# Two linear-attention units per batch feeding an ELU feed-forward layer: block 0's exponentials in place, block 1's in four slots, unit 3's loads ahead of the last quarter of W2, and a new written order up to the fourth block

## The chip, the cores and the metric

The kernel runs on one core of a Trainium2 chip. The figure that counts is the device time of one execution in microseconds: the median of three runs of the kernel before is 292.26 us (292.03 to 292.69). All inputs and the output are float32.

Engine names: PE is the matrix engine, PEld its weight loads, ACT the scalar engine (exponentials, copies, relu), DVE the vector engine, POOL the GpSimd engine, SP the engine that only issues transfers. POOL issues transfers too, between its own computations.

## The reference

```python
q_s = exp(q - max(q, -1));  q_s = q_s / sum(q_s, -1)
k_s = exp(k - max(k, 2));   k_s = k_s / sum(k_s, 2)
kv  = einsum('bhsd,bhse->bhde', k_s, v)
x   = einsum('bhsd,bhde->bhse', q_s, kv)      # 8 batches, 8 heads, 576 rows, 64 wide
x   = x.transpose(0, 2, 1, 3).reshape(4608, 512)
h   = x @ w_in                                # 512 x 2048
g   = where(h > 0, h, exp(min(h, 0)) - 1)
out = g @ w_out                               # 2048 x 512
```

## The kernel before, in words

The work has two halves that run at the same time. The attention half goes in 16 **units** (n = 0 to 15); a unit is half the heads of one batch (`load`). It loads q, k and v (576 KB each), takes exponentials on ACT, row sums and reciprocals of q on DVE, the scaled q (`QS`) on POOL or DVE, turns `QS` on PE (`tp`, line 457) for units 0 to 3 or by a transposing transfer (`turn`, line 470) for later ones, multiplies k and v on PE (`kv_mm`, line 507), scales the result into `MBLK` (lines 516, 520) and multiplies again (`ao_parts`, line 550, for units 0 and 1; `ao_mm`, line 538, later). Two copies (`xt`, line 277) put the product into `XT`, the transposed input of the feed-forward half.

The feed-forward half goes in nine **blocks** of 512 tokens (j = 0 to 8). A block's first product (GEMM1, `hg_mm`, line 620) has eight groups g of eight 128x512 matmuls; each group needs its columns of `W1` and fills a pair of PSUM banks, `PS0` to `PS3`. Then `hg` forms the ELU: one ACT exponential of 1024 columns (line 646), and either an ACT relu (648) and a DVE pass (652), or two DVE passes (657, 659). The second product (`out_mm`, line 673) uses `W2` for blocks 0 and 1; blocks 2 to 8 use a seven-product form of it (lines 757, 733 and 806).

In block 0 only, GEMM1's first three groups go quarter by quarter, kc = 0 to 3: kc 0 and 1 need `XT` of unit 0, kc 2 and 3 that of unit 1. `W1` comes in seven transfers on POOL's queue (`load_w1`, line 377): one for each kc of groups 0 to 2 (384 KB), groups 3, 4 and 5 (512 KB each), groups 6 and 7 (1 MB). `W2` comes in four quarters of 1 MB (`load_w2`, line 385).

What sets the order: the program records every operation once, with what it reads and writes; `ORDER` is a table written out by hand or by a solver, one line of operation numbers for each engine, and every engine does its line strictly in that order. A transfer stands in the line of the engine that issues it. Waits on semaphores are derived from reads and writes, so an operation that waits holds everything behind it in its line. `fill` adds spare matmuls on the identity (`spare`, line 892) into the planned gaps of PE ahead of the first GEMM1; each group of them waits for the identity and for the ACT or DVE operation that by the plan ends last before the gap begins.

In blocks 0 and 1 the exponential of a group goes into one of two slots (`ESB`), taken in turn by a counter (`eslot`); the slot is free again when DVE has made `GR` from it. From block 2 on the exponential is written where the result will stand (`GE` is the same memory as `GR`, with another type). The slots lie in the memory that later holds differences of `W2` (`TB`, made by `combos`).

## Time and profile before

| what | value |
|---|---|
| profiled execution, first to last instruction | 290.4 us |
| median of the three timed runs | 292.26 us |
| PE busy | 280.6 us |
| DVE busy | 225.5 us |
| ACT busy | 209.7 us |
| POOL busy | 167.8 us |
| granted PE clock, mean | 0.999 |
| transfers between 5 and 40 us | 355 to 400 GB/s |

The profile gives no time of its own for the profiled execution beyond its span, 290.4 us; the median of the timed runs is 1.9 us more than that. PE is the busiest engine, and the chain of work that ended last runs through PE from 13.8 us to 287.1 us. Busy time of ACT, DVE and POOL counts only where PE waits for them. PSUM results of a matmul come after the start of the next one, so in a timeline a group of matmuls overlaps with the one behind it; the chain gives times that add up.

### The profile page before, as it was taken

The page shows a single profiled execution, that of the slowest core. Times are in us where ns is not written, and L with a number is a line of the kernel's source. Part 1 is how long each engine was busy: PE and PEld are TensorE (multiplying, and loading weights), DVE is VectorE, ACT ScalarE, POOL GpSimd, SP SyncE. Part 2 cuts the span into 40 slices and gives each one's busy share as a digit, 9 for nine tenths or more (in the row PEclk, how much of TensorE's full clock was granted, in tenths as well). Part 3 has the DMA queues.
Part 4 walks back from the last instruction along what each step waited for, and adds up shares of the span by engine and source line. Part 5 has one row for each costly group of instructions (what it writes and reads, how often), then busy time and mean ns, then how long its engine had stood idle before and what let it go on. Part 6 is the DMA issues. An engine that isn't in the chain of part 4 may idle for free.

```text
span 290.4 us, 5465 instructions
## 1 busy us (share of the span) xinstructions
PE 280.6 (97%) x2176; PEld 243.7 (84%) x2176; DVE 225.5 (78%) x425; ACT 209.7 (72%) x237; POOL 167.8 (58%) x161
## 2 busy tenths in 40 slices
PE   2899999999999999999999999999999999999995
PEld 0488787778888899989999988989999999988995
DVE  3758834777699978989996987688977786794884
ACT  4857839989899899968995598975385656665510
POOL 1991335523869778676574886757314234277741
PEclk9999999999999999999999999999999999999999
DMA  7999999798896838739939295313102002300334
GB/s 259 399 363 390 389 389 339 163 260 323 238 349 163 241 91 228 202 78 305 178 96 222 56 292 129 76 40 71 46 18 56 0 2 67 78 2 1 92 73 128
DMA packets 36474, 50.04 MB, mean 172 GB/s; under 512 B 16352, under 2 KB 18144, under 8 KB 36448
## 3 DMA queue, kind: packets, MB, share of 16 engines
q1 hardware_dynamic: 29680, 33.96, 43.7%
q0 software_dynamic: 6528, 15.47, 17.8%
q8 instruction: 17, 0.28, 0.5%
q10 hardware_dynamic: 240, 0.26, 0.3%
q14 instruction: 9, 0.07, 0.1%
HBM read 36.70 MB, written 9.44 MB: 159 GB/s over the span
## 4 chain that ended last, share of the span: by engine, by line
PE 94%; DMA 2%; POOL 2%; SPq 0%; issue 0%; DVE 0%
PE PS L620 46%; PE PS L806 32%; PE PS L673 10%; PE PS L538 3%; DMA KR<-in_k_dram 2%; PE PS L507 2%; POOL W L377 1%; POOL VB L277 0%; PE PS L457 0%; POOL QS L433 0%; SPq L359 0%; PE PS L550 0%; DVE OSB L815 0%
## 5 line engine op out<-in xcount | busy, mean ns | idle before, releaser
L620 PE MATMUL PS<-XT,W 128*128 128x512 f32 x576 | 142.0, 393 | 0.1
L620 PEld LDWEIGHTS PS<-XT,W 128*128 128x128 f32 x576 | 105.0, 188 | 21.2 <-DVE GR L659 0.5
L652 DVE SCALAR_TENSOR_TENSOR GR<-PS,GE 128x512 fp32r<-128x512 f32 x112 | 76.8, 686 | 18.7 <-ACT GE L648 16.7
L646 ACT ACTIVATE GE<-PS 128x1024 f32<-128x1024 f32 x56 | 57.4, 1025 | 40.0 <-PE PS L620 34.2
L757 POOL TENSOR_TENSOR GR<-GR 128x256 fp32r<-128x256 f32 (+1 forms) x48 | 47.2, 996 | 31.5 <-DVE SB L757 16.6
L648 ACT ACTIVATE GE<-GE 128x1024 f32<-128x1024 f32 x56 | 59.4, 1061 | 1.4
L806 PE MATMUL PS<-W,GR 128*128 128x256 f32 x336 | 53.7, 283 | 0.0
L806 PE MATMUL PS<-TB,GR 128*128 128x256 f32 x336 | 51.3, 283 | 0.0
L806 PEld LDWEIGHTS PS<-W,GR 128*128 128x128 f32 x336 | 47.6, 191 | 1.7
L806 PEld LDWEIGHTS PS<-TB,GR 128*128 128x128 f32 x336 | 45.7, 191 | 0.7
L433 POOL TENSOR_TENSOR QS<-QR,RZQ 128x1152 f16<-128x1152 f32 (+1 forms) x16 | 30.4, 1898 | 21.4 <-DVE RZQ L423 19.7
L815 DVE TENSOR_TENSOR OSB<-OSB,PS 128x256 f32<-128x256 f32 x84 | 34.7, 416 | 10.3 <-PE PS L806 9.2
L673 PE MATMUL PS<-W,GR 128*128 128x512 f32 x128 | 32.7, 396 | 0.0
L757 POOL TENSOR_TENSOR GR<-SB,GR 128x256 fp32r<-128x256 f32 (+1 forms) x18 | 17.3, 971 | 24.6 <-PE PS L806 12.7
L673 PEld LDWEIGHTS PS<-W,GR 128*128 128x128 f32 x128 | 23.3, 188 | 5.0 <-DMA W<-in_moe_w_out_dram 0.5
L757 POOL TENSOR_TENSOR SB<-GR 128x256 fp32r<-128x256 f32 (+1 forms) x20 | 19.2, 965 | 13.7 <-DVE GR L652 6.4
L421 DVE TENSOR_REDUCE ZQ<-QR 128x18 f32<-128x1152 f32 (+2 forms) x18 | 21.7, 1207 | 6.1 <-ACT QR L419 4.8
L757 DVE TENSOR_TENSOR GR<-GR 128x256 fp32r<-128x256 f32 (+1 forms) x36 | 21.3, 603 | 0.6 <-PE PS L806 0.6
L277 POOL CAST VB<-VR 128x1152 bf16<-128x1152 f32 (+1 forms) x11 | 11.9, 1084 | 13.1 <-DMA VR<-in_v_dram 13.1
L646 ACT ACTIVATE ESB<-PS 128x1024 f32<-128x1024 f32 x16 | 16.1, 1024 | 4.5 <-PE PS L620 3.4
L399 ACT ACTIVATE KR<-KR 128x1152 bf16<-128x1152 f32 x16 | 18.4, 1155 | 0.8 <-DMA KR<-in_k_dram 0.8
L277 ACT ACTIVATE XT<-PS 128x512 fp32r<-128x512 f32 (+6 forms) x23 | 13.6, 595 | 6.3 <-PE PS L538 3.2
(58 smaller groups left out, 271.4 us busy)
## 6 DMA issues: line engine op xcount, KB each, us to landing
out_dram<-OSB SPq DMA_DIRECT2D x61, 128.0 KB, 2.4
QR<-in_q_dram SPq DMA_DIRECT2D x12, 576.0 KB, 4.9
KR<-in_k_dram SPq DMA_DIRECT2D x12, 576.0 KB, 6.3
VR<-in_v_dram SPq DMA_DIRECT2D x12, 576.0 KB, 5.1
W<-in_moe_w_out_dram POOLq DMA_DIRECT2D x4, 1024.0 KB, 16.7
QR<-in_q_dram POOLq DMA_DIRECT2D x4, 576.0 KB, 12.1
VR<-in_v_dram POOLq DMA_DIRECT2D x4, 576.0 KB, 13.0
KR<-in_k_dram POOLq DMA_DIRECT2D x4, 576.0 KB, 11.1
```

The source lines that it names most:

```text
L277: return e.activation(dst, src, AF.Copy) if e is self.nc.scalar else e.tensor_copy(dst, src)
L399: S.add("act", t_act(1152, False), lambda e: e.activation(ek[:, :, :, :].rearrange("p h c d -> p (h c d)"), flat(k), AF.Exp), key - 2, X=[ ...
L421: S.add("dve", t_dve(m), lambda e, qp=qp, zp=zp: e.tensor_reduce(zp, qp, AX.X, ALU.add), key - 3, R=[f"qR{i}{x}" for x in xs], W=[f"ZQ{i}{ ...
L433: lambda e, qp=q[:, :, a:b, :], rz=rz, dst=qs[:, :, a:b, :]: e.tensor_tensor(dst, qp, rz, ALU.mult),
L620: last = e.matmul(P[:, t * 512:(t + 1) * 512], self.W1[:, kc, tt * 128:(tt + 1) * 128], self.XT[:, kc, rc:rc + BLK], start=(kc == 0), stop ...
L646: S.add("act", t_act(1024, True), lambda e: e.activation(ge, P, AF.Exp), key, W=own, X=banks)
L648: S.add("act", t_act(1024, False), lambda e: e.activation(ge, ge, AF.Relu, bias=1.0, scale=-1.0), key, X=own)
L652: S.add("dve", t_dve(512 if j else 1024), lambda e, u=u: e.scalar_tensor_tensor(*(x[:, :, u, :] if j else x for x in (gt, P)), 0.0, ge[:, ...
L673: last = e.matmul(dst, self.tile(jb, jj, ts), self.W2[:, jj, c0:c1], start=(jj == 0), stop=(jj == 15))
L757: lambda e: e.tensor_tensor(dst, a, b, op), key, R=R, W=W, X=X, after=after)
L806: last = e.matmul(dst, a[i][:, y_, :], b[i][:, y_, :], start=start and i == 0 and y_ == 0, stop=stop and i == len(grps) - 1 and y_ == z - ...
L815: S.add("dve", t_dve(256), lambda e: e.tensor_tensor(dst, a, b, ALU.add), key, R=R, W=W, X=X, after=after)
```

## The change

Five things change in the program, and the table of orders is new up to about the end of block 1 (behind it the table is the old one with every number raised by 4).

1. `hg`: block 0's exponentials, and those of block 1's groups 4 to 7, are written in place into `GE`; block 1's groups 0 to 3 have a slot of their own each (`ESB` has four slots of 4 KB instead of two). Where a place in `GE` still held parts of units 1 and 3 (`early`), the exponential waits for their last readers (`after=users`). `combos` names the two new slots as written.
2. `load_w2` takes any range of `W2`; the loads of unit 3's k and v are recorded ahead of the last quarter of `W2`, which comes in two transfers of 512 KB. `out_mm` of block 0 does the last quarter in two halves.
3. Groups 4 and 5 of `W1` come in one transfer of 1 MB.
4. Unit 3's turn and first product use the bank pair `AB` (PS3), as the other units do; before they used `C` (PS2).
5. `spare_until` is the second `kv_mm` itself.

```diff
-        if j == 1:
-            gw += sorted(set(sum((self.early(u) for u in us), [])))
+        lent = [n for u in us for n in self.early(u)] if j == 1 else []
+        users = [o for n in sorted(set(lent)) for o in S.w.get(n, []) + S.r.get(n, [])]
...
-        own = gw
-        if j < 2:
-            i = self.eslot % 2
-            self.eslot += 1
-            own = [f"E{i}"]
-            ge = self.ESB[i][:, :].rearrange("p (c u t) -> p c u t", c=2, u=2) if j else self.ESB[i][:, :]
-        S.add("act", t_act(1024, True), lambda e: e.activation(ge, P, AF.Exp), key, W=own, X=banks)
+        own, apart = gw, j == 1 and g < 4
+        if apart:
+            own = [f"E{g}"]
+            ge = self.ESB[g][:, :].rearrange("p (c u t) -> p c u t", c=2, u=2)
+        S.add("act", t_act(1024, True), lambda e: e.activation(ge, P, AF.Exp), key, W=own, X=banks, after=users)
...
-        for g0, g1 in ((3, 4), (4, 5), (5, 6), (6, 8)):
+        for g0, g1 in ((3, 4), (4, 6), (6, 8)):
             self.load_w1(g0, g1, range(4), -30)
...
-        self.load_w2(2, -27)
-        self.load_w2(3, -25)
+        self.load_w2(8, 12, -27)
         for t in "kv":
             self.load(3, t, -26)
+        for jj in (12, 14):
+            self.load_w2(jj, jj + 2, -25)
...
-            ps, eng = (C if x == 0 else AB, "both") if n == 3 else (AB, "act")
+            ps, eng = AB, "both" if n == 3 else "act"
...
-                self.out_mm(0, ts, (ts + 2) % 4, 4 * jq, 4 * jq + 4, key)
+                for jj in range(4 * jq, 4 * jq + 4, 2 if jq == 3 else 4):
+                    self.out_mm(0, ts, (ts + 2) % 4, jj, jj + (2 if jq == 3 else 4), key)
...
     "pe": (
-        "35 52 33 37 56 57 54 60 80 78 79 64 65 82 81 84 87 85 88 83 86 89 99 103 110 133 121 107 "
+        "32 34 36 51 55 53 56 59 78 79 80 82 63 64 81 83 84 87 85 88 86 89 99 103 110 133 121 107 "
```

**The first place is PE from its first instruction to the first GEMM1 matmuls.** `PS0<-ID` are the spare matmuls, `QS0` and `QS1_54` the scaled q of units 0 and 1, `VB0,KR0` the `kv_mm` of unit 0. Before:

```order
L892 MATMUL PS0<-ID 128x512 x5
L457 MATMUL PS3<-ID,QS0 128x128 x4
L892 MATMUL PS0<-ID 128x512 x2
L457 MATMUL PS1<-ID,QS1_54 128x128 x5
L892 MATMUL PS0<-ID 128x512
L457 MATMUL PS3<-ID,QS0 128x128 x5
L507 MATMUL PS2<-VB0,KR0 64x65 x36
L892 MATMUL PS0<-ID 128x512 x4
L550 MATMUL PS2<-qsT0,MBLK0 128x512 x2
L457 MATMUL PS1<-ID,QS1_54 128x128 x4
L507 MATMUL PS0<-VB1,KR1 64x65 x36
L620 MATMUL PS2<-XT,W1 128x512 x2
```

After:

```order
L890 MATMUL PS0<-ID 128x512 x6
L457 MATMUL PS3<-ID,QS0 128x128 x5
L890 MATMUL PS0<-ID 128x512 x4
L457 MATMUL PS3<-ID,QS0 128x128 x4
L507 MATMUL PS2<-VB0,KR0 64x65 x36
L457 MATMUL PS1<-ID,QS1_54 128x128 x5
L890 MATMUL PS0<-ID 128x512 x5
L550 MATMUL PS2<-qsT0,MBLK0 128x512
L457 MATMUL PS1<-ID,QS1_54 128x128 x4
L550 MATMUL PS2<-qsT0,MBLK0 128x512
L507 MATMUL PS0<-VB1,KR1 64x65 x36
L620 MATMUL PS3<-XT,W1 128x512 x2
```

Unit 0 is turned as a whole ahead of unit 1, the larger half first; there are 15 spare matmuls instead of 12, and the first group of them waits for the small exponential on ACT that loads the table (line 343) where before it waited for an exponential of unit 0's q. On ACT, the copy of unit 0's second half of `qsT` stands behind the exponential of unit 1's k and the cast of unit 1's v; before, the copies of `qsT` stood ahead of both.

**The second place is POOL's line from the third transfer of W1 on.** Before:

```order
L377 DMA W1<-in_moe_w_in_dram 128x1x768 x2
L377 DMA W1<-in_moe_w_in_dram 128x4x256
L433 TENSOR_TENSOR QS1_54<-QR1,RZQ1 128x2x4x64
L277 CAST VB1<-VR1_56 128x2x4x64
L377 DMA W1<-in_moe_w_in_dram 128x4x256 x2
L377 DMA W1<-in_moe_w_in_dram 128x4x512
L385 DMA W2<-in_moe_w_out_dram 128x4x512
L359 DMA QR0<-in_q_dram 128x2x576
L385 DMA W2<-in_moe_w_out_dram 128x4x512
L359 DMA QR1<-in_q_dram 128x2x576
L359 DMA VR0<-in_v_dram 128x2x576
L359 DMA KR0<-in_k_dram 128x2x576
```

After:

```order
L377 DMA W1<-in_moe_w_in_dram 128x1x768
L433 TENSOR_TENSOR QS1_54<-QR1,RZQ1 128x2x4x64
L359 DMA QR0<-in_q_dram 128x2x576
L377 DMA W1<-in_moe_w_in_dram 128x1x768
L277 CAST VB1<-VR1_56 128x2x5x64
L377 DMA W1<-in_moe_w_in_dram 128x4x256
L377 DMA W1<-in_moe_w_in_dram 128x4x512 x2
L359 DMA VR0<-in_v_dram 128x2x576
L385 DMA W2<-in_moe_w_out_dram 128x4x512
L433 TENSOR_TENSOR QS0<-QR0,RZQ0 128x2x5x64
L385 DMA W2<-in_moe_w_out_dram 128x4x512
L359 DMA KR0<-in_k_dram 128x2x576
```

Unit 2's q is now loaded ahead of the last quarter of `W1`'s first groups (kc 2 comes last), and its v ahead of `W2`; the second quarter of `W2` stands behind a product on POOL that waits for unit 2's reciprocals.

**The third place is ACT in block 0**, from the last copy of `XT` of unit 1 on. `ESB0` and `ESB1` are the two slots, `GE` the memory of the results. Before:

```order
L277 ACTIVATE XT<-PS0 128x512
L646 ACTIVATE ESB0_57<-PS3 128x1024
L646 ACTIVATE ESB1_58<-PS1 128x1024
L648 ACTIVATE ESB1_58<-ESB1_58 128x1024
L646 ACTIVATE ESB0_57<-PS2 128x1024
L646 ACTIVATE ESB1_58<-PS0 128x1024
L648 ACTIVATE ESB1_58<-ESB1_58 128x1024
L646 ACTIVATE ESB0_57<-PS3 128x1024
```

After:

```order
L277 ACTIVATE XT<-PS0 128x512
L395 ACTIVATE QR0<-QR0 128x1152
L644 ACTIVATE GE_50<-PS3 128x1024
L644 ACTIVATE GE_50<-PS1 128x1024
L646 ACTIVATE GE_50<-GE_50 128x1024
L644 ACTIVATE GE_50<-PS2 128x1024
L644 ACTIVATE GE_50<-PS0 128x1024
L644 ACTIVATE GE_50<-PS3 128x1024
L646 ACTIVATE GE_50<-GE_50 128x1024
```

No exponential waits for a slot any more, the relu of group 3 comes behind the exponential of group 4, and the exponential of unit 2's q stands at the front. SP's line is the same in both kernels.

More of the change, by code (lines that the diff above doesn't have):

```diff
@@ L318, in alloc @@
         self.ESB = [at(f"ESB{i}", [128, 1024], F32, offset=tbase + NSP * 1024 + 4096 * i)
-                    for i in range(2)]
+                    for i in range(4)]
         self.OSB0 = [at(f"OSBX{i}", [128, 512], F32, offset=tbase + 2048 * i)
@@ L718, in w2 @@
         z0, z1 = GROUPS[grp]
-        return [f"W2_{s}" for s in range(z0 // 2, (z1 + 1) // 2)]
+        return [f"W2_{s}" for s in range(z0, z1)]
     def combos(self, key, grp):
```

32 lines of the change are left out of this document (16 added, 16 removed), and 136 rows, old and new, of the table ORDER.

## The prediction

> **What bounds the kernel now.** I read the page's busy line and its chain by engine first, then the chain piece by piece, then the first 20 us as a timeline, and last the times from issue to landing of single transfers.
>
> ```profile
> PE 280.6 (97%) x2176; PEld 243.7 (84%) x2176; DVE 225.5 (78%) x425; ACT 209.7 (72%) x237; POOL 167.8 (58%) x161
> PE 94%; DMA 2%; POOL 2%; SPq 0%; issue 0%; DVE 0%
> ```
>
> PE is busy for all but 10 us of the span, and 94% of the chain that ended last is PE. So the end moves by three things only: when PE begins the real work, what it waits for afterwards, and the tail. The pieces of the chain that tell this (start, length, line, number of matmuls):
>
> ```profile
> 13.79 0.49 PE PS L507 x35
> 14.27 1.59 PE PS L620 x6
> 15.86 0.46 PE PS L550 x2
> 16.32 13.16 PE PS L620 x58
> 29.48 0.37 PE PS L538 x4
> 29.85 1.93 PE PS L673 x8
> ...
> 31.80 3.06 PE PS L673 x12
> 34.86 0.52 PE PS L457 x9
> ...
> 39.19 1.05 PE PS L673 x4
> ...
> 42.63 3.67 PE PS L673 x16
> ...
> 48.44 5.57 PE PS L620 x24
> ...
> 54.05 2.11 PE PS L620 x8
> ...
> 58.95 3.91 PE PS L620 x16
> ...
> 74.73 1.81 PE PS L620 x8
> ...
> 271.45 15.60 PE PS L806 x130
> ```
>
> The long pieces give the price of work without waits: 13.16/58 = 0.227 us for a GEMM1 matmul, 3.67/16 = 0.229 us for one of the second product. Against these prices some pieces are too long: the first 20 of line 673 took 1.93 + 3.06 = 4.99 instead of 4.58 (0.41 lost), the four at 39.19 1.05 instead of 0.92 (0.13), the 32 from 48.44 5.57 + 2.11 = 7.68 instead of 7.26 (0.42), the 16 at 58.95 3.91 instead of 3.63 (0.28). Together 1.24 us. From 74.73 on a group of eight takes 1.81 = 8 x 0.227; I find no more waits of PE up to the last piece. The order there is the old one, so a shift of PE at 73 us is carried to the end. What can be won is therefore 1.24 us of waits plus what the beginning gives. The beginning:
>
> ```profile
> 2.03 0.20 ACT L343 ACTIVATE RZK<-RZK 128x2 f32<-128x2 f32 x1
> 4.82 1.26 ACT L419 ACTIVATE QR<-QR 128x512 f32<-128x512 f32 x2 [2.59 <-DMA QR<-in_q_dram]
> 5.49 0.69 DVE L421 TENSOR_REDUCE ZQ<-QR 128x8 f32<-128x512 f32 x1 [3.88 <-ACT QR L419]
> 5.51 2.32 PE L892 MATMUL PS<-ID 128*128 128x512 f16 x5 [5.51 <-ACT QR L419]
> 6.49 1.05 POOL L433 TENSOR_TENSOR QS<-QR,RZQ 128x512 f16<-128x512 f32 x1 [4.62 <-DVE RZQ L423]
> 8.04 1.06 PE L892 MATMUL PS<-ID 128*128 128x512 f16 x2
> 8.93 0.58 ACT L277 ACTIVATE qsT<-PS 128x512 fp32r<-128x512 f16 x1
> 9.39 0.87 POOL L277 CAST VB<-VR 128x512 bf16<-128x512 f32 x1
> 10.19 1.91 POOL L377 DMA_DIRECT2D W<-in_moe_w_in_dram  x3
> 10.82 1.04 PE L892 MATMUL PS<-ID 128*128 128x512 f16 x4
> 12.01 1.17 POOL L433 TENSOR_TENSOR QS<-QR,RZQ 128x512 f16<-128x512 f32 x1
> 12.35 0.73 PE L550 MATMUL PS<-qsT,MBLK 128*128 128x512 f32 x2 [0.49 <-DVE MBLK L520]
> 13.40 0.60 ACT L277 ACTIVATE XT<-PS 128x512 fp32r<-128x512 f32 x1
> ```
>
> And the transfers: two rows in the timeline that issue (start, length), and the answers that give the time from issue to landing of the one transfer in that stretch, in the same order.
>
> ```profile
> 3.58 0.52 SPq L359 DMA_DIRECT2D VR<-in_v_dram  x1
> 17.26 0.80 POOL L385 DMA_DIRECT2D W<-in_moe_w_out_dram  x1
> ```
> ```profile
> VR<-in_v_dram SPq DMA_DIRECT2D x1, 576.0 KB, 8.8
> W<-in_moe_w_out_dram POOLq DMA_DIRECT2D x1, 1024.0 KB, 14.5
> W<-in_moe_w_in_dram POOLq DMA_DIRECT2D x1, 512.0 KB, 6.4
> KR<-in_k_dram POOLq DMA_DIRECT2D x1, 576.0 KB, 4.8
> ```
>
> So unit 1's v lands at 3.58 + 8.8 = 12.4, and the second quarter of W2 at 17.26 + 14.5 = 31.8, just where the chain's piece of twelve begins at 31.80: that is the wait at W2. The third answer is group 5 of W1, the middle one of three issues from
>
> ```profile
> 13.56 2.28 POOL L377 DMA_DIRECT2D W<-in_moe_w_in_dram  x3
> 15.00:20.00 5.00, 5.00 (x23) 4.13 (x22) 1.60 (x3) 2.42 (x3) 5.00 (x8) 1.00 1.75 355
> 20.00:25.00 5.00, 5.00 (x23) 4.13 (x22) 4.60 (x6) 4.68 (x6) 3.23 (x5) 1.00 1.40 388
> ```
>
> issued at 13.56 + 0.76 = 14.3 and landed at 20.7. The two other rows are windows; their last figure is GB/s. The queue is never empty here, so a transfer lands when the bytes ahead of it have passed, at 355 to 388 GB/s: 576 KB cost 1.5 us, 1 MB 2.7. The fourth answer is a load of k at 46 us, when the queue had run low: 4.8 us for bytes worth 1.5, so up to 3.3 us go from issue to first bytes.
>
> **Term 1, the beginning.** GEMM1 starts when both unit 0's XT and unit 1's kv_mm are done. ACT now stands so: unit 1's k, unit 1's v (half of it, 512 columns), then unit 0's second qsT, then XT. The v lands at 12.4 and nothing of that chain can be earlier: cast 0.62 (the mean of the two at 4.82), 13.05; qsT 0.58 (row at 8.93), 13.6; line 550's first matmul needs 0.1 to start and its result is there after 0.73 - 0.23 = 0.5, 14.25; XT 0.60, 14.85; 0.1 to PE: 14.95. Before, the qsT copies lay ahead of the v and XT was ready at 14.0. On POOL: reduce, reciprocal and scaling of the larger half of unit 0 (640 columns, 1.05 x 640/512 = 1.3) end at 8.0; two issues of W1 and the first cast end at 10.25 as before (the cast waits for v, not for them); one issue 0.64 (1.91/3), unit 1's QS 1.05, two issues 1.35 end at 13.3; the cast of 640 columns costs between 0.87 (the row of 512) and 1.09 (that times 640/512), so 14.2 to 14.4, and kv_mm 0.49 behind it ends at 14.7 to 14.9. Both chains meet at 14.95 against 14.27: **0.7 later**, between 0.3 (POOL's cast at its lowest and half of ACT's handovers gone) and 1.7 (the clock, below). Some of the 0.23 that the first six matmuls lost behind kv_mm (1.59 instead of 1.36) should now lie in the wait for XT: 0.1 off.
>
> **Term 2, waits that go.** In block 0 the exponentials and in block 1 the slots no longer wait for DVE; unit 3's k and v come early enough that nothing in 38 to 48 us waits for them; the last quarter of W2 comes in halves. With this the 0.13, 0.42 and 0.28 go: 0.83 us. They were lost in the copies and slots ahead of block 1's first groups, and I follow the new order by hand to 73 us without a wait above 0.1 (the copies of XT behind unit 3's reduce, the turn of unit 3 behind a copy of PS3: 0.1 together). Bounds: nothing to all of it.
>
> **Term 3, transfers that now come later.** Ahead of W2's second quarter now pass unit 2's q (as before) and its v (new): 31.8 + 1.5, less 0.25 for 1 MB of W1 in longer rows (1 MB at 388 instead of 355), makes 33.0. PE wants it at 14.95 + 64 x 0.227 + 0.46 + 0.37 + 8 x 0.229 + 0.52 = 32.65 (blocks 0's GEMM1, two small products, eight matmuls, a turn). So of the 0.41 lost there before, 0.35 stay. Its issue on POOL stands behind the scaling of unit 2's q, which needs a reciprocal that DVE does behind group 1: 25.1 by the same prices, and the bytes ahead of it last until 28.5, and its own come by 25.1 + 3.3 = 28.4, so the queue just doesn't run dry. Groups 4 and 5 of W1 in one transfer, with unit 2's q ahead: 20.7 + 1.5 - 0.25 = 21.95; PE wants group 4 at 14.95 + 32 x 0.227 + 0.46 = 22.65. Before, group 4 had its own transfer and some 3 us in hand; now it has 0.7. A transfer can land later than its bytes say, so this costs nothing to 0.7; I take nothing. The relu of group 3 behind the exponential of group 4 lets PS0 go at 27.9, wanted at 28.15: nothing.
>
> **Term 4.** The cast and copies that move from ACT to DVE cost PE nothing, since DVE has idle time up to 80 us; two more bank uses by unit 3 are in term 2.
>
> **The sum.** +0.7 - 0.1 - 0.83 + 0.1 - (0.41 - 0.35) = -0.2 us: a span of 290.2 against the profiled 290.4, and as the median is 1.9 us above the span, 292.1 against 292.26. A measurement of this kernel can tell about 0.2%, 0.58 us, from no change; this is less.
>
> [...] The spare matmuls before took 0.46 us each at 5.51 and 0.53 at 8.04, and 0.26 at 10.82: PE reaches its full rate between 2.5 and 5.3 us after it begins. After the change the first six wait only for the ACT row that ends at 2.23, run to 5.0, and then PE has nothing until QS at 8.0. Counted from there, full rate comes between 10.6 and 13.4. At the slow rate the five spare matmuls ahead of line 550 run from 12.3; with full rate at 13.4 they end at 13.9 instead of 13.6, and 0.25 is lost, most of which W2's second quarter hides. If it doesn't come before line 550 at all, the five end at 12.3 + 5 x 0.46 = 14.6, line 550 and kv_mm run slow as well (some 0.2), and GEMM1 starts at 16.1; that is rival c. [...]
>
> **The rivals.** (a) *The beginning isn't later.* If the handovers on ACT are shorter and the cast on POOL is at its low price, GEMM1 starts at 14.6, and the transfers are early enough: -0.7, 291.5. For it: every wait in term 1 is 0.05 to 0.1 that I put in. Against: v at 12.4 is fixed. (b) *W1 and W2 late; slower.* Group 4 waits for the joined transfer, or POOL's line holds W2's second quarter behind QS; it decides when the joined transfer lands after 22.65. With 23.5 and a queue that runs dry for 0.5: +0.8, 293.1. For it: group 5 landed 6.4 us after issue, and the transfers wait in one queue; against: the later ones have their bytes in hand. (c) *PE still at half rate when line 550 comes*: GEMM1 at 16.1 instead of 14.95, of which 0.35 is hidden by W2: -0.2 + 0.8 = +0.6, 292.9. Against: the four spare matmuls and the turns behind 8.0 leave PE hardly idle, and 5.3 us sufficed before. (d) *The waits don't go*: what was lost in block 1 wasn't the slots, and 0.7 comes back: 292.8.
>
> **How the numbers follow.** Forecast 0.45 (its own range 291.7 to 292.6), a 0.25, b 0.13, c 0.09, d 0.08. Faster than 291.68 is a and a little of the forecast, 0.28; slower than 292.84 is b, half of c and d, and what I didn't see in an order that is new on all engines: 0.27; the rest, 0.45, is the same. The range takes a at its best (start at 14.6, all 1.24 gone: 291.1) and b at 293.2.
>
> **What would show it.** In the profile of the changed kernel: the first spare matmul at about 2.3 us; the first L620 at 14.9 to 15.2; the first piece of second products beginning at 30.4 and a wait of 0.3 to 0.4 behind the turn of unit 2 at about 33; the first GEMM1 of block 1 at about 48.4; 24 of it without a wait; the same last piece of 130 and the same tail. A first L620 beyond 15.5, a wait ahead of group 4, or pieces in 50 to 62 us that are too long would prove me wrong.

## The result: 293.28 us, slower by 0.31%

| | kernel before | changed kernel |
|---|---|---|
| median, us | 292.15 (291.82 to 292.69, 8 runs) | 293.28 (292.56 to 293.59, 8 runs) |
| ratio | | 1.0031, 95% interval 1.0020 to 1.0042 |
| span of the profiled execution, us | 290.4 | 290.8 |

Predicted were 292.1 us, with a range of 291.1 to 293.2; the time lies just above the range. The execution of the changed kernel that was profiled is the shortest of its eight: the others have spans of 290.9 to 291.8. So its profile shows 0.4 us of the loss of 1.1, and the rest has to be found in what differs from one execution to the next.

The busy line of the page of the changed kernel; PE and DVE are busier than before by 1.1 and 4.5 us, ACT less by 3.5:

```profile
PE 281.7 (97%) x2179; PEld 244.6 (84%) x2179; DVE 230.0 (79%) x430; ACT 206.2 (71%) x231; POOL 171.1 (59%) x162
```

The pieces of its chain (start, length, line, matmuls) that answer to those shown of before. Line 672 is the second product, line 805 the later form of it:

```profile
14.80 8.31 DMA W<-in_moe_w_in_dram
...
23.25 7.55 PE PS L620 x32
...
31.17 1.93 PE PS L672 x8
...
33.61 2.82 PE PS L672 x12
...
49.03 1.86 PE PS L620 x8
50.89 0.47 PE PS L672 x2
51.36 5.44 PE PS L620 x24
...
58.86 2.07 PE PS L620 x8
...
271.79 15.60 PE PS L805 x130
```

Before, 58 matmuls of GEMM1 ran from 16.32 to 29.48 without a break. Now the chain doesn't reach back through PE at 23.25 but into a transfer: the joined one of W1's groups 4 and 5, issued at 14.8 and landed at 23.11. Behind it everything is tight: the second products without a lost 0.4 us (2.82 for twelve), 24 matmuls of block 1 in 5.44 = 24 x 0.227. The last piece begins 0.34 us later than before (271.45), and so it ends.

The first 24 us as a timeline (start, length, engine, line; in brackets the idle time and what ended it):

```profile
2.29 2.74 PE L890 MATMUL PS<-ID 128*128 128x512 f16 x6 [2.29 <-ACT RZK L343]
8.08 0.71 PE L457 MATMUL PS<-ID,QS 128*128 128x128 f16 x5 [3.05 <-POOL QS L433]
12.01 1.54 PE L890 MATMUL PS<-ID 128*128 128x512 f16 x5
14.91 2.12 PE L620 MATMUL PS<-XT,W 128*128 128x512 f32 x8
23.25 7.55 PE L620 MATMUL PS<-XT,W 128*128 128x512 f32 x32 [0.30 <-DMA W<-in_moe_w_in_dram]
```

GEMM1 begins at 14.91, 0.64 later than before. Its first 32 matmuls and line 550 end PE's work at 14.91 + 32 x 0.227 + 0.46 = 22.65 or so; group 4 begins at 23.25, 0.6 later. By the starts of the single matmuls PE was ready at 22.78, so the wait and the slower matmul behind it cost 0.5 to 0.6 us.

### The profile page after: what moved, and what is told of

It is laid out like the page before. It is cut to its first block, busy times and chain, and to the rows that moved or that the text cites. A ratio compares the mean times of both kernels' runs of the same rounds, so it can differ in the third digit from the quotient of the medians.

```text
span 290.8 us, 5462 instructions
## 1 busy us (share of the span) xinstructions
PE 281.7 (97%) x2179; PEld 244.6 (84%) x2179; DVE 230.0 (79%) x430; ACT 206.2 (71%) x231; POOL 171.1 (59%) x162
## 4 chain that ended last, share of the span: by engine, by line
PE 91%; DMA 4%; POOL 3%; DVE 1%; issue 0%; ACT 0%; POOLq 0%
PE PS L620 43%; PE PS L805 32%; PE PS L672 10%; DMA W<-in_moe_w_in_dram 3%; PE PS L538 3%; PE PS L507 2%; DMA QR<-in_q_dram 1%; POOL W L377 1%; POOL QS L433 1%; POOL VB L277 1%; PE PS L457 0%; DVE ZQ L421 0%; ACT QR L419 0%; DVE OSB L814 0%; POOL QR L359 0%
## 5 line engine op out<-in xcount | busy, mean ns | idle before, releaser
L620 PE MATMUL PS<-XT,W 128*128 128x512 f32 x576 | 142.2, 393 | 0.3 <-DMA W<-in_moe_w_in_dram 0.3
L620 PEld LDWEIGHTS PS<-XT,W 128*128 128x128 f32 x576 | 105.0, 188 | 21.2 <-issue 0.7
L650 DVE SCALAR_TENSOR_TENSOR GR<-PS,GE 128x512 fp32r<-128x512 f32 (+1 forms) x120 | 84.4, 704 | 22.6 <-ACT GE L646 20.6
L644 ACT ACTIVATE GE<-PS 128x1024 f32<-128x1024 f32 x68 | 69.5, 1025 | 46.1 <-PE PS L620 40.3
L646 ACT ACTIVATE GE<-GE 128x1024 f32<-128x1024 f32 x62 | 65.8, 1061 | 1.6
L433 POOL TENSOR_TENSOR QS<-QR,RZQ 128x1152 f16<-128x1152 f32 (+2 forms) x17 | 32.7, 1926 | 19.5 <-DVE RZQ L423 17.7
L756 POOL TENSOR_TENSOR GR<-SB,GR 128x256 fp32r<-128x256 f32 (+1 forms) x18 | 17.4, 974 | 24.4 <-PE PS L805 12.7
L277 POOL CAST VB<-VR 128x1152 bf16<-128x1152 f32 (+2 forms) x11 | 12.7, 1157 | 12.1 <-DMA VR<-in_v_dram 9.2
L395 ACT ACTIVATE QR<-QR 128x1152 f32<-128x1152 f32 x14 | 16.2, 1159 | 3.0 <-DMA QR<-in_q_dram 3.0
L277 ACT ACTIVATE OSB<-PS 128x256 f32<-128x256 f32 (+1 forms) x21 | 7.9, 387 | 13.6 <-PE PS L805 13.6
```

The costliest lines, as they stand in the source:

```text
L277: return e.activation(dst, src, AF.Copy) if e is self.nc.scalar else e.tensor_copy(dst, src)
L433: lambda e, qp=q[:, :, a:b, :], rz=rz, dst=qs[:, :, a:b, :]: e.tensor_tensor(dst, qp, rz, ALU.mult),
L620: last = e.matmul(P[:, t * 512:(t + 1) * 512], self.W1[:, kc, tt * 128:(tt + 1) * 128], self.XT[:, kc, rc:rc + BLK], start=(kc == 0), stop ...
L644: S.add("act", t_act(1024, True), lambda e: e.activation(ge, P, AF.Exp), key, W=own, X=banks, after=users)
L646: S.add("act", t_act(1024, False), lambda e: e.activation(ge, ge, AF.Relu, bias=1.0, scale=-1.0), key, X=own)
L650: S.add("dve", t_dve(512 if j else 1024), lambda e, u=u: e.scalar_tensor_tensor(*(x[:, :, u, :] if j else x for x in (gt, P)), 0.0, ge[:, ...
```

## The experiments

All times are medians, each compared with runs of the kernel before on the same chip (medians of 292.01 to 292.12). "Before" and "changed" stand for the two kernels.

### Again, and the spare matmuls

The changed kernel once more, without an edit.

> The changed kernel once more, for a second profile beside the first, whose span of 290.8 us is the shortest of its eight runs (median about 291.5). Theory W (the joined transfer of W1's groups 4 and 5 lands after PE wants it, and by how much differs from run to run): a profile with a longer span shows it landing after 23.1, the wait ahead of line 620's 33rd matmul beyond 0.6 us, and the same first L620 at 14.9. Theory C (the early spare matmuls leave PE idle from 5 to 8 us, and the full rate comes at another moment from run to run): the longer span goes with a lower granted clock, slow 128x512 matmuls (over 0.4 us) later than 13 us and a first L620 at 15.3 to 16. Median time by both 293.0 to 293.5.

Measured: 293.31 us (292.62 to 294.24), ratio 1.0041 [1.0026, 1.0057]; the profiled span is 291.1. The two rows of its chain:

```profile
14.82 8.60 DMA W<-in_moe_w_in_dram
...
23.55 7.58 PE PS L620 x32
```

The first L620 came at 14.93, as in the first profile; the joined transfer landed 0.3 us later, and the span is 0.3 longer. That is what theory W expected.

Next, the spare matmuls of the changed kernel late, as before had them, and those of before early, as the changed kernel has them. In both the edit is the planner's start of the spares:

```diff
-    SPIN_FROM, WARM = 5400.0, 11300.0
+    SPIN_FROM, WARM = 5600.0, 11300.0      # changed kernel, spares late
...
-    SPIN_FROM, WARM = 5400.0, 11300.0
+    SPIN_FROM, WARM = 5200.0, 11300.0      # kernel before, spares early
```

> The changed kernel with its first spare matmuls (five instead of six) behind the first exponential of unit 0's q, as in the kernel before, so that they run from 5.6 to 7.9 us and PE is hardly idle ahead of the first turn at 8.1. Theory C: full rate from about 10.2 us in every run, the spare matmuls at 8.6 take 0.26 us and not 0.46, the spans agree within 0.3 us and the median falls by 0.5 to 0.8 us to 292.5 to 292.8. Theory W: the time stays at 293.1 to 293.4, since GEMM1 begins at 14.9 because of unit 1's v either way and its group 4 still waits.

> The kernel before with its first five spare matmuls behind the small table-loading exponential that ends at 2.2 us, as in the changed kernel: they run from 2.3 to 4.6, then PE is idle to 7.6. Theory C: full rate comes at 12 to 14 us in place of 10.2, later in some runs, GEMM1 begins 0.2 to 1.0 us later and the median rises by 0.3 to 0.9 us to 292.5 to 293.1 with a wider spread. Theory W: no change, 292.0 to 292.3.

Measured: 293.11 us (292.61 to 293.43), ratio 1.0030 [1.0020, 1.0040], for the late spares in the changed kernel; 292.00 us (291.86 to 292.25), ratio 0.9997 [0.9988, 1.0006], for the early ones in before. The timelines of the two, in this order:

```profile
5.84 2.31 PE L890 MATMUL PS<-ID 128*128 128x512 f16 x5 [5.84 <-ACT QR L419]
24.18 7.55 PE L620 MATMUL PS<-XT,W 128*128 128x512 f32 x32 [0.72 <-DVE GR L650]
```
```profile
2.29 2.31 PE L892 MATMUL PS<-ID 128*128 128x512 f16 x5 [2.29 <-ACT RZK L343]
14.14 1.66 PE L620 MATMUL PS<-XT,W 128*128 128x512 f32 x6
```

In before the early spares leave PE idle from 4.6 to 7.55 and GEMM1 begins at 14.14 all the same. So early spares alone cost nothing. In the changed kernel the late spares don't help: the seven runs have granted clocks of 0.998 or more, and the time is 293.11 us. In the 14 executions of the changed kernel the span doesn't follow the granted clock closely either: 290.8 to 292.4 us at 0.998 and more, 290.9 to 292.0 at 0.994, 291.8 and 291.9 in the two at 0.988, where the clock may have a part. As the cause of the loss theory C falls. With the late spares group 4 began as late as 24.18. The row names a DVE pass that ended at 24.10, but that pass freed the bank of group 1, which group 4 doesn't use; the joined transfer, issued at 15.0, landed 9.0 us later, at the same moment.

### The transfers in the changed kernel

W1's groups 4 and 5 apart again:

```diff
-        for g0, g1 in ((3, 4), (4, 6), (6, 8)):
+        for g0, g1 in ((3, 4), (4, 5), (5, 6), (6, 8)):
```

> The changed kernel with W1's groups 4 and 5 in two transfers of 512 KB again. Theory W: group 4 lands by 22.2 us, the wait ahead of it (0.58 us in the profile: 23.25 instead of 22.67) goes; W2's second quarter, landed at 32.7, is then wanted at 33.0, so the gain stays: 292.3 to 292.8 and the time stands 0.5 to 1.0 us below the changed kernel. Theory C: the time doesn't move by more than 0.2 us where the clock came late, and by 0.5 only where it didn't; median 293.0 to 293.3.

Measured: 293.05 us (292.35 to 294.74), ratio 1.0035 [1.0020, 1.0050]. The wait ahead of group 4 is gone, and the time hardly moved. The chain shows why (line numbers are lower by 2 here), and below it stand POOL's rows of the same time:

```profile
17.55 7.46 PE PS L618 x32
...
25.03 1.04 ACT GE L642
...
26.09 1.60 DVE GE L653
27.69 1.14 DVE GR L648
...
28.87 2.12 PE PS L618 x8
```
```profile
25.65 0.81 POOL L383 DMA_DIRECT2D W<-in_moe_w_out_dram  x1
26.45 0.72 POOL L357 DMA_DIRECT2D KR<-in_k_dram  x1
27.16 0.74 POOL L357 DMA_DIRECT2D QR<-in_q_dram  x1
```

The last group of GEMM1 wants the bank of group 3. That is free only when DVE has made group 3's result, and DVE does it behind its pass of group 4 (line 653), which waits for group 4's exponential. That pass took 1.60 us here, against 0.68 in before, while POOL issued three transfers one behind the other. From 17.55 to the end of the last group, 28.87 + 2.12 = 30.99, the 56 matmuls took 13.4 us instead of 56 x 0.227 = 12.7. By the starts of the single matmuls 0.36 us of that are lost ahead of the last group, and 0.15 each ahead of the matmuls at 18.33 and 26.70, which begin right behind landings of W1 (18.29 and 26.57). So a wait of 0.6 us stood in front of others of 0.7, half of it at the bank. The next two kernels put group 3's relu and pass back ahead of group 4's, alone and with the split:

```diff
-    act: ... 96 100 104 101 111 112 ...      dve: ... 98 105 102 106 113 ...
+    act: ... 96 100 101 104 111 112 ...      dve: ... 98 102 105 106 113 ...
```

> The changed kernel with block 0's relu of group 3 on ACT ahead of the exponential of group 4 again, and DVE's pass of group 3 ahead of that of group 4, as in the kernel before. Theory B (two waits lie behind each other in block 0: the joined W1 transfer ahead of group 4, and behind it the bank of group 3, which group 6 wants 24 matmuls later and which is free only 5.3 us after group 4 begins, since the relu of group 3 stands behind group 4's exponential): alone this changes little, since in the changed kernel's profile the bank is free at 28.6 and wanted at 28.7; 0 to 0.3 us less, 293.0 to 293.3. Theory H (the head alone: GEMM1 begins 0.64 us later, and this is carried to the end): no change, 293.2 to 293.4.

> Both at once: W1's groups 4 and 5 in two transfers, and group 3's relu and pass in their old places. Theory B: with the transfers split alone 0.7 us were lost at the bank (58 matmuls' stretch of 12.9 us took 13.6), with both edits no wait is left in block 0's GEMM1, the second products begin at about 30.5 instead of 31.17, and the time falls by 0.5 to 0.9 us to 292.3 to 292.7. Theory H: 293.0 to 293.2, as with the transfers split alone.

Measured: alone 293.32 us (292.87 to 294.40), ratio 1.0045 [1.0027, 1.0062]; both edits 292.69 us (292.36 to 293.29), ratio 1.0018 [1.0008, 1.0028]. This is what theory B expected of the times: each edit alone gives 0 to 0.25, both together 0.6. The interval of both still overlaps those of the changed kernel (1.0020 to 1.0042, and 1.0026 to 1.0057), so the size of the gain is uncertain. The chains of the two:

```profile
14.79 8.86 DMA W<-in_moe_w_in_dram
...
23.78 7.51 PE PS L620 x32
```
```profile
17.70 0.91 PE PS L618 x4
...
18.65 8.46 PE PS L618 x36
...
27.13 3.90 PE PS L618 x16
```

Theory B expected no wait in GEMM1 with both edits, and that isn't so in the execution that was profiled (span 291.2, above the usual 290.9 of this kernel): the pieces at 18.65 and 27.13 begin behind landings of W1, at 18.61 and 26.99, and cost 0.3 us each. The bank isn't waited for any more.

Four profiles so far have group 4 waiting for the joined transfer in the changed kernel's order of transfers. From one to the other the span follows the start of group 4:

| kernel | group 4 begins | span |
|---|---|---|
| changed, first profile | 23.25 | 290.8 |
| changed, again | 23.55 | 291.1 |
| group 3's relu first | 23.78 | 291.3 |
| spares late | 24.18 | 291.6 |

From 22.65, where PE would have been ready in the first profile, this is 0.6 to 1.5 us (in the last two, GEMM1 itself began 0.2 later). The changed kernel's usual span is 291.5. That group 4 begins near 24 us in such a run is read off this table, since none of them was profiled.

### The head pulled forward

Could the 0.64 us of the later beginning be won back? On ACT the copy of unit 0's second qsT ahead of unit 1's k, on POOL the cast of unit 1's v ahead of two issues; once in the changed kernel, once with the two edits above:

```diff
-    act: ... 21 33 22 37 39 35 57 ...      gp: ... 17 47 67 16 38 18 ...
+    act: ... 21 33 22 35 37 39 57 ...      gp: ... 17 47 38 67 16 18 ...
```

> The changed kernel with its head alone pulled forward: on ACT the copy of the second half of unit 0's qsT ahead of the exponential of unit 1's k (it can run at 10.95 instead of 12.9), on POOL the cast of unit 1's v ahead of the issues of unit 2's q and of W1's third quarter (12.45 instead of 13.4). By both theories the first L620 comes at 13.9 to 14.3 instead of 14.91. Theory H: the time falls by 0.5 to 0.8 us to 292.4 to 292.8. Theory B: group 4 then waits the longer for the joined transfer, which isn't earlier (23.1 to 24.0 us, later by up to 0.6 by the later issue), and the time stays at 293.0 to 293.5.

> All three edits: the head pulled forward, W1's groups 4 and 5 in two transfers, group 3's relu and pass in their old places. Theory B: group 4's own transfer (landed at about 22.1 with the transfers split) is now wanted at 21.9 and holds PE up to 0.4 us, and W2's second quarter (32.7 to 33.0) is wanted at 32.3; so the gain over the two edits without the head is 0.1 to 0.4 us: 292.0 to 292.5. Theory H: the head gives its whole 0.6 to 0.9 us: 292.2 to 292.5 from the head alone, whatever the others do.

Measured: 294.08 us (293.47 to 295.63), ratio 1.0078 [1.0053, 1.0103], and 294.32 us (293.01 to 296.64), ratio 1.0086 [1.0058, 1.0115]: both slower, by more than either theory said. The first one's timeline:

```profile
14.55 2.12 PE L620 MATMUL PS<-XT,W 128*128 128x512 f32 x8 [0.60 <-DMA W<-in_moe_w_in_dram]
...
19.96 10.27 PE L620 MATMUL PS<-XT,W 128*128 128x512 f32 x44 [1.91 <-DMA W<-in_moe_w_in_dram]
```

The edit delayed the issue of the last quarter of W1's groups 0 to 2 by 1.2 us (12.85 to 14.03), and it landed 2.0 us later (17.90 to 19.92); PE now waited 1.91 for it. The transfers ran short meanwhile: 147 GB/s between 15 and 16 us, against 349 in the changed kernel. So PE's pace through GEMM1 hangs on when W1 is issued. Theory H is not tested by this, since the edit that pulled the head forward pushed W1 back.

### The moved transfers in the kernel before

The direct test: the two moves of transfers done in the kernel before, and nothing else. Numbers of operations are those of before.

```diff
-    gp: ... 48 40 19 20 21 69 68 70 ...      ((3, 4), (4, 5), (5, 6), (6, 8))
+    gp: ... 48 40 68 19 20 21 69 70 ...      unit 2's q (68) ahead of W1's groups 4 to 7: q alone
+    ((3, 4), (4, 6), (6, 8))                 groups 4 and 5 in one transfer: joined alone
```

> The kernel before with two of the change's moves of transfers alone: unit 2's q is issued ahead of W1's groups 4 to 7, and groups 4 and 5 come in one transfer. Theory Q (the queue: bytes put ahead of W1 and the joined transfer make group 4 late, by how much differs from run to run): group 4 is wanted at 22.0 us, the joined transfer lands between 22.0 and 23.5, the time rises by 0.2 to 1.2 us to 292.3 to 293.3 and the runs scatter over 1 us instead of 0.4. Theory H (the late head): no change, 291.9 to 292.2.

> The kernel before with unit 2's q issued ahead of W1's groups 4 to 7, groups 4 and 5 still apart. Theory Q1 (it is the sum of both moves that uses up group 4's slack of about 2.5 us: 1.5 us for q's bytes, 1.3 us for the half of the joined transfer): group 4 alone is still in time or nearly so: 292.0 to 292.5, 0 to 0.4 us above before. Rival Q2 (q ahead is enough by itself, the joining does nothing): 292.9 to 293.3, as with both.

> The kernel before with W1's groups 4 and 5 in one transfer, unit 2's q behind W1. Theory Q1: the joined transfer lands at 20.7 to 21.7, wanted at 22.0: 291.9 to 292.4. Rival Q3 (the joining is enough by itself): 292.8 to 293.3.

| moved in the kernel before | median, us | ratio |
|---|---|---|
| both | 293.13 (292.59 to 293.99) | 1.0035 [1.0024, 1.0046] |
| unit 2's q ahead | 292.70 (292.13 to 293.52) | 1.0021 [1.0011, 1.0032] |
| groups 4 and 5 joined | 292.06 (291.73 to 292.55) | 0.9997 [0.9987, 1.0006] |

The timelines of the three, in this order:

```profile
23.31 7.55 PE L617 MATMUL PS<-XT,W 128*128 128x512 f32 x32 [0.77 <-DMA W<-in_moe_w_in_dram]
```
```profile
22.74 3.87 PE L618 MATMUL PS<-XT,W 128*128 128x512 f32 x16 [0.41 <-DMA W<-in_moe_w_in_dram]
26.85 3.95 PE L618 MATMUL PS<-XT,W 128*128 128x512 f32 x16 [0.24 <-DMA W<-in_moe_w_in_dram]
```
```profile
16.08 13.34 PE L617 MATMUL PS<-XT,W 128*128 128x512 f32 x58
```

Both moves together cost 1.04 us in a kernel that has none of the rest of the change, as much as the whole change lost. That the two figures agree is chance: in the changed kernel the later beginning adds 0.64, and the stretch behind 31 us gives 0.98 back. Unit 2's q is the larger part: it makes group 4 late by 0.41 and the last transfer, of groups 6 and 7, by 0.24. The joining alone is free, and costs some 0.4 once q stands ahead (the two intervals overlap). Q1 holds in that; its 0 to 0.4 for q alone was too small. The trace keeps sixteen landings of each transfer; with q alone fifteen of those of group 4's transfer had come at 20.77, in time, and the last came at 22.60 (group 4 began at 22.74).

### Unit 2's q put back in the changed kernel

Three attempts to have the change without the early q. The first two take the order of before up to about 37 us, the second with the changed kernel's head; the third only puts q behind groups 4 and 5 (with the split and the relu as above) and moves its exponential, reciprocal, scaling and turn behind it.

```diff
-    gp: ... 67 16 38 18 19 20 71 68 119 69 ...
+    gp: ... 16 39 18 19 20 21 69 68 70 73 72 71 ...     (numbers with the split)  second; the first is the same from 19 on
+    gp: ... 16 39 18 19 20 68 21 72 69 70 120 ...       (numbers with the split)  third
```

> The changed program with W1's groups 4 and 5 apart, and the order of the kernel before up to about 37 us (PE to the kv_mm of unit 2, POOL to the cast of unit 2's v, with unit 2's q behind W1 and behind W2's first quarter); behind it the changed order. GEMM1 begins at 14.3. Theory Q: no wait in block 0's GEMM1, second products at 29.85 as before, then the gain of block 1 (0.67 us) stays: 291.2 to 291.7, runs within 0.4 us. Theory H gives the same here. If the changed order's gain in block 1 hangs on its early loads of unit 2, it is gone: 292 to 292.6.

> As the one before, but with the changed kernel's head (PE to the end of groups 0 to 2, ACT and DVE to the copies of unit 1's XT, POOL to W1's last transfer), from which only the load of unit 2's q is taken out and put behind W1. GEMM1 begins at 14.9. Theory Q: W1's transfers land 1.5 us or more earlier, no wait ahead of group 4, second products at 30.5, runs within 0.5 us: 291.8 to 292.3, half a microsecond above the hybrid because of the head. Theory H (the head and not the transfers makes the changed kernel slow): 292.8 to 293.2.

> The changed kernel with W1's groups 4 and 5 apart, group 3's relu in its old place, and unit 2's q issued behind groups 4 and 5 (its exponential behind group 3's relu, its reciprocal behind group 4's pass, its turn behind eight more matmuls, the issue of W2's second quarter ahead of its scaling). GEMM1 begins at 14.9 to 15.2. Theory Q1: W1's groups 3 to 5 land some 1.5 us earlier, the small waits that the two edits alone left in block 0's GEMM1 (0.3 to 0.6 us in that profile) go, and the time falls from 292.69 to 292.0 to 292.4, the 0.64 us of the late head being paid for by the gain in block 1. Theory H (the head): 292.6 to 293.0. If unit 3's chain becomes late by the later unit 2, a wait appears between 38 and 48 us and the time is above 293.

Measured: 295.50, 295.37 and 298.03 us (ratios 1.0107, 1.0111 and 1.0194, intervals no wider than 0.0025 to either side). The chain of the second and the waits of PE (total, times, longest) in the third:

```profile
17.97 12.70 PE PS L618 x56
...
46.93 5.15 DMA QR<-in_q_dram
```
```profile
PE PS L505 <- POOL VB L275: 2.2, 1, 2.2
PE PS L670 <- DVE GR L648: 1.2, 1, 1.2
```

In the second, 56 matmuls of block 0 take 12.70 = 56 x 0.227: with the changed kernel's head, W1 split, group 3's relu in its old place and q behind W1 nothing in GEMM1 waits. But the loads of later units stand on POOL behind products that wait for units 2 and 3, and these now come late; the third waits 2.2 us for a cast that stands behind them. The totals say nothing about the head or the transfers. They show that these orders need q early; one written anew for a late q was not tried.

### The parts of the change in block 1

The slots alone in the kernel before, in before's order (two copies of `combos` on POOL change places):

```diff
-        own = gw
-        if j < 2:
-            i = self.eslot % 2
+        own, apart = gw, j == 1 and g < 4
+        if apart:
+            own = [f"E{g}"]
...
-                    for i in range(2)]
+                    for i in range(4)]
```

> The kernel before with the first part of the change alone: block 0's exponentials in place, block 1's groups 0 to 3 in four slots, groups 4 to 7 in place; order of before (two copies of combos on POOL change places, since they now write one slot's name). If the 0.42 us lost in the 32 matmuls from 48.44 and the 0.28 at 58.95 are waits for a slot, as the second term of the prediction has it, they go and the time falls by 0.5 to 0.8 us to 291.3 to 291.6, with no wait taking their place. If what was lost there hung on the order and not on the slots, no change: 291.9 to 292.2.

Measured: 291.84 us (291.62 to 292.60), ratio 0.9992 [0.9981, 1.0002]. The chain:

```profile
48.56 5.60 PE PS L620 x24
...
54.18 2.14 PE PS L620 x8
...
59.09 3.68 PE PS L620 x16
```

Of the 0.28 us at 58.95 all but 0.05 are gone (3.68 for sixteen), the 0.42 in the 32 matmuls ahead of them stay (5.60 + 2.14 = 7.74): they were no wait for a slot. In the changed kernel they are gone (1.86 + 5.44 for 32), where block 1's first group stands ahead of two of the last matmuls of block 0. So that was tried as well, on top of the slots: the last four matmuls of block 0 behind the first half of block 1's first group, then behind both halves, with their copy on ACT later.

```diff
-    pe: ... 177 159 178 172 165 192 194 191 193 ...    act: ... 198 185 188 173 166 224 249 250 ...
+    pe: ... 177 159 172 165 192 178 194 191 193 ...    act: ... 198 185 173 166 188 224 249 250 ...    first
+    pe: ... 177 159 172 165 192 194 178 191 193 ...    act: ... 198 185 173 166 224 249 188 250 ...    second
```

> The kernel before with the first part of the change (slots) and one move in block 1: the last four matmuls of block 0's second product stand behind the first half of block 1's first group, their copy on ACT behind the copies of unit 3's XT. The 0.42 us that the slots alone left in the 32 matmuls from 48.4 is a wait for the copies of unit 3's product and for the bank of group 1; with 0.9 us of other work ahead of it, it goes: 291.3 to 291.7, below both kernels. If the wait only moves (to the half of group 1 that needs unit 3's XT): 291.8 to 292.1.

> The slots alone in the kernel before, with the last four matmuls of block 0's second product behind block 1's first group (both halves), and their copy on ACT behind that group's exponential. With the slots alone the last eight of the 32 matmuls from 48.4 began 0.3 us late, behind the pass that frees the bank of group 1, 5.8 us after that group began, and the 24 ahead of them lost 0.16. If the order of block 1 is what is left of the change's gain, group 1 now begins 0.9 us earlier beside the same work, the bank is free in time, and the time falls by 0.2 to 0.5 us below the slots alone (291.84): 291.3 to 291.6. If the move makes group 1 wait for unit 3's XT instead: 291.8 to 292.3.

Measured: 293.27 us (293.08 to 293.68), ratio 1.0038 [1.0025, 1.0051], and 292.36 us (292.10 to 293.31), ratio 1.0008 [0.9998, 1.0018]. The waits of PE in the first (total, times, longest), and the chain of the second:

```profile
PE PS L536 <- DVE MBLK L518: 0.9, 1, 0.9
PE PS L618 <- DVE GR L648: 0.7, 1, 0.7
```
```profile
47.79 0.18 DVE RZK L516
...
49.45 1.85 PE PS L620 x8
...
52.21 5.44 PE PS L620 x24
```

In the second the 0.42 are gone (1.85 + 5.44), but the four matmuls had also covered DVE's work on unit 3's `MBLK`, and PE now waits there 0.9 us. No version beat before by more than the slots alone, whose interval still reaches 1.

### A later head in the kernel before

On ACT, the copy of unit 0's second qsT behind the exponential of unit 1's k:

```diff
-    act: ... 45 53 34 38 39 58 ...
+    act: ... 45 53 38 34 39 58 ...
```

> The kernel before with its head made later alone: on ACT the copy of the second half of unit 0's qsT stands behind the exponential of unit 1's k. GEMM1 begins at 14.5 to 14.9 instead of 14.2; the transfers aren't touched. Term 1 of the prediction (a later beginning is carried to the end, less what W2's second quarter hides): the time rises by what GEMM1 is later, less up to 0.4: 292.1 to 292.6. If instead a later head is hidden altogether, since the waits behind it shrink by as much: 291.9 to 292.1.

Measured: 292.59 us (291.89 to 292.97); the ratio over the rounds is 1.0005 [0.9994, 1.0015], so the runs don't settle it. The chain:

```profile
14.75 1.67 PE PS L620 x6
...
30.41 1.93 PE PS L673 x8
...
59.53 3.92 PE PS L620 x16
```

Here GEMM1 began 0.48 later than in the profile of before (14.27), the second products 0.56 later (29.85), and the piece at 59 us 0.58 later (58.95). In this execution a later beginning is carried on whole.

## Why the prediction was wrong

**The beginning (term 1) was right.** GEMM1 at 14.95 was forecast and 14.91 measured, in the second profile 14.93: v, cast, second qsT, line 550 and XT came as worked out. The fear in the paragraph on PE's full rate, and rival c with it, were borne out only in small. The first spares began at 2.29 as said, PE had nothing from 5.0 to 8.1, and still the five at 12.01 took 1.54 us (0.46 each would be 2.3), so the full rate came in the middle of them. The clock's own record has it from 12.60 on in this profile, from 11.71 in the second, and from 13.50 in the kernel with group 3's relu first, where the five took 1.99 us and GEMM1 began at 15.10, 0.2 later. That is close to the 0.25 which the paragraph worked out for a full rate at 13.4. That the count starts anew at 8.0 was the author's estimate: the three profiles have the full rate 3.6 to 5.4 us behind 8.1. Early spares in the kernel before cost nothing (292.00). A fall of the clock stands in the profile of the kernel with W1 split: full rate from 5.27 on, a granted clock of 0.50 from 8.69 to 12.10, full rate again behind it. PE had been idle for 3.1 us before (5.03 to 8.14), and GEMM1 began at 14.95 all the same. No run shows what brought the fall about.

**Term 2 was right in size and half wrong in cause.** The second products began at 31.17 instead of 29.85, 1.32 later (0.64 from the beginning, the rest from the wait ahead of group 4), block 1's first group at 49.03 instead of 48.44, 0.59 later, and the last piece of 130 at 271.79 instead of 271.45, 0.34 later. So the stretch behind 31 us gave back 0.98 us: the 0.83 forecast for the waits and the 0.41 that before lost at W2 would make 1.24, so that 0.26 came back as small new waits, where 0.1 was forecast. But the slots alone remove only 0.23 of it, in the sixteen matmuls at 58.95; the 0.42 in block 1's first 32 matmuls go with the order of block 1.

**Term 3 holds the step that failed: "Groups 4 and 5 of W1 in one transfer, with unit 2's q ahead: 20.7 + 1.5 - 0.25 = 21.95; PE wants group 4 at 22.65 [...] I take nothing."** PE wanted it at 22.65 (22.78 by the starts of the matmuls). It landed at 23.11 in the shortest execution and at 23.42 and 23.64 in two other profiles, so the 0.7 us in hand were used up in all of them. The wait cost 0.5 to 0.6 us in the first profile, 0.8 to 0.9 in the second and, by the table above, more in the usual execution. The bytes were not the error. Of the sixteen landings that the trace keeps of this transfer, the middle one came at 21.85, 21.83 and 21.76 in the three profiles, where 21.95 was forecast, and the fifteenth at 22.65, 22.38 and 22.04, in time. But group 4 began only behind the last one (23.11 and 23.25, 23.42 and 23.55, 23.64 and 23.78), and that came 0.5, 1.0 and 1.6 us behind the fifteenth. So what failed is the estimate that "a transfer lands when the bytes ahead of it have passed": it gave the middle one of the landings. That "a transfer can land later than its bytes say" stands in the same place, with a price of nothing to 0.7, and the sum took nothing, without a row that gave a reason. That the transfers before group 4 had the slack to lose is shown in the kernel before, where both moves cost 1.04 us, q ahead alone 0.69 and the joining alone nothing.

The figure of 20.7 that the sum starts from couldn't show this. It is the last landing of group 5, whose first and last lay 0.56 us apart. The transfer right behind it, of groups 6 and 7, has 1.93 us between them, and its row in the kernel before (the last figure is from issue to landing) is:

```profile
W<-in_moe_w_in_dram POOLq DMA_DIRECT2D x1, 1024.0 KB, 9.7
```

Issued at 15.10 it landed at 24.8, where its bytes alone give 20.7 + 2.7 = 23.4. The same 1.4 us on top of 21.95 would have put the landing 0.7 behind the moment at which PE wants it.

Take the 0.6 out of the first profile's span and 290.2 are left, which is the span that was forecast (W2's second quarter, landed 7.3 us after its issue at 25.44, would still have been in time). That is arithmetic, though: the kernel with W1 split shows that other waits took the place of this one.

**A second step of term 3 failed unseen: "The relu of group 3 behind the exponential of group 4 lets PS0 go at 27.9, wanted at 28.15: nothing."** The last group found that bank free only at 28.83 when group 4's transfer was in time, because DVE's pass of group 4 took 1.60 us instead of 0.68. In the changed kernel the late transfer hides this. With both mended the time is 292.69, 0.6 below the changed kernel.

**The part on W2's second quarter** (0.35 us of wait at 33) could not be seen: PE came there at 33.61, after it had landed.

**The rivals.** (b) is what happened: a wait ahead of group 4, which decides when the joined transfer lands after 22.65, priced at 293.1, measured 293.28 (its second half, the queue that runs dry, is not needed). It had 0.13; a slack of 0.7 us against transfers that wait in one queue deserved more. (a) was not the case, and (c) only by the 0.2 us of one profile. (d) was right about the 0.42, which wasn't the slots, but the time didn't come back: in the new order these waits went all the same. The sign that was named, "a wait ahead of group 4", stands in the profile.

**What stays open.** Of the 1.1 us, some 0.6 come back when the transfers are split and the bank is freed earlier. For the remaining 0.6 above before (292.69 against 292.06) there is the profile of one execution, in which two landings of W1 cost 0.3 us each. Unit 2's q stood ahead of W1 there too, and in before it costs 0.69 by that alone, but the changed kernel without it could not be measured, since unit 2 then comes too late for the new order. And no run was made in which the last landings of the transfers come earlier.

## What to carry to other kernels

When a transfer is put ahead of others in a queue that is never empty, list every later transfer with the moment it is wanted, and set against it the last landing and not what the bytes give: here the last of the sixteen came 1.3 to 1.9 us behind the middle one, and a later transfer in the same profile of before already showed it. Price the joining of two transfers together with what is put ahead of them: here it cost nothing by itself (ratio 0.9997), and some 0.4 us (293.13 against 292.70) once unit 2's q stood ahead. When an edit that removes a proven wait doesn't move the time, look for the next wait behind it (here a bank that was freed too late) before giving up the cause. And where runs of one kernel scatter more than those of another, profile it more than once: the start of one group gave the span from run to run.

## What the runs showed of the hardware

**Landing.** The joined transfer landed 8.3, 8.6 and 8.9 us after its issue in three profiles with the same head, and by the bytes ahead of it 7.2 were expected. The trace keeps sixteen landings of each transfer. Those of the joined one lie between 21.49 and 23.11 in the first profile, and group 4 began at 23.25.

**A packet of instructions among the weights.** In the first profile of the changed kernel and in that of before, the distance from a transfer's first landing to its last jumps once up to 36 us, where a 16 KB packet of the instruction queue stands. In the changed kernel it is 0.64 us for the transfer that landed at 17.90 and 1.59 for the next, at 20.37; the packet took from 17.56 to 18.51. In before it is 0.56 us for the one at 20.78 and 1.93 for the next, at 24.81; the packet took from 20.88 to 22.01. The rows of the two windows, changed kernel first:

```profile
q8 instruction: 1, 0.02, 5.4%
```
```profile
q8 instruction: 1, 0.02, 5.5%
```

In both it stays at its new size up to 36 us. At the next such packet it rises in the changed kernel (39.77 to 40.87) from 1.61 to 2.53, and stays at 1.9 in before (40.19 to 41.29). No run moves a packet, so it isn't shown that the packets are the cause.

**DVE beside POOL's issues.** The pass over 128x1024 float32 in place took 0.68 us in before and 1.60 in the kernel with W1 split, where it began in the midst of three transfers that POOL issued from 25.65 to 27.90. In the changed kernel's two profiles it took 1.07 and 0.79. In these three POOL was issuing the load of k (`KR`) when the pass began or while it ran, and the pass ended 0.51 to 0.53 us behind the end of that issue (26.95 and 27.48, 27.02 and 27.53, 27.17 and 27.69), however early it had begun. In the kernel with the late spares it began only 0.05 us before that issue ended and took 0.69. In before the same pass of an earlier group took 0.69 at 22.39, while POOL issued a load of v (22.37 to 23.23). No run shows what makes the pass longer.
